# A decode kernel of attention and a token mixer: the query weights in four loads at the head of the queue

## The chip, the core and the metric

The kernel runs on one core of one Trainium2 chip. A core has engines with instruction lists of their own: TensorE (PE in the profile; its weight loads are PEld), VectorE (DVE), ScalarE (ACT), GpSimd (POOL) and SyncE (SP). Sixteen DMA engines bring data from the chip's memory (HBM) into the on-chip memory SBUF, which has 128 rows, here called partitions. A load is issued by one engine's instruction (here nearly always SP's), is split into one packet for each row of its target, and increments a semaphore when it has landed. The engines wait on semaphores for each other.

The metric is the device time of one execution, in microseconds (us). The kernel before takes a median of 1266.54 us in 3 runs (1265.91 to 1266.6).

## What is computed

One decoding step: a row `x` of 448 numbers goes through attention over a long cache and, beside it, through a small mixer; a gate mixes the two.

```python
def _A_ref(x, k_cache, v_cache, wq, wo):        # 16 query heads, 8 key heads, 65536 keys, 256 wide
    q = (x @ wq).reshape(B, Sq, Hq, Dh).transpose(0, 2, 1, 3)
    k = jnp.repeat(k_cache, rep, axis=1)
    v = jnp.repeat(v_cache, rep, axis=1)
    scores = jnp.einsum("bhqd,bhkd->bhqk", q, k) * (Dh ** -0.5)
    p = _softmax(scores, axis=-1)
    o = jnp.einsum("bhqk,bhkd->bhqd", p, v)
    return o.transpose(0, 2, 1, 3).reshape(B, Sq, Hq * Dh) @ wo
...
g = _sigmoid((x * gate_w).sum(-1, keepdims=True))
a = _A_ref(x, A_k_cache, A_v_cache, A_wq, A_wo)
b = _B_ref(x, B_w1, B_b1, B_w2, B_b2)           # layer norm, 448 x 1792 mixer with gelu
return g * a + (1 - g) * b
```

All inputs are bf16. The two caches hold 268 MB each and are read once. The query weights `A_wq` are 448 x 4096 (3.67 MB), the output weights `A_wo` 4096 x 448 (3.67 MB).

## The kernel before

The keys and values are cut into NP = 32 blocks of 16,384 positions, four for each of the 8 key heads. A block of keys or of values is 8.39 MB: 128 partitions of 64 KB. Keys go to a ring `kring` of one and a half blocks, values to one buffer `vbuf`. For each block, PE transposes the keys (L348) into PSUM, VectorE and ScalarE copy them back to SBUF (L656, L796), PE multiplies them by the query (L369), the maximum and the exponential follow, and PE multiplies the weights by the values (L400).

All large loads are on SP's list, in an order written out by hand (L251 to L315), and so go through one queue:

1. `load_wo(0)` (L253, L257): the output weights of the first head pair, 448 KB in 128 rows of 3.5 KB. PE reads them first in `project` (L461), after the first head's four blocks.
2. The big part of the query weights, `wq_a` (L258): rows 0 to 383 of `A_wq`. WF = 3 rows of it go to one partition, so it is 128 rows of 24 KB, 3072 KB. Its place in SBUF is the front of `vbuf`, which the values take over later.
3. The rest of the query weights, `wq_b` (L260): 64 rows of `A_wq`, each cut in two, 128 rows of 4 KB, 512 KB.
4. The first block of keys, in two halves of 4096 KB (L266, L267).
5. From then on values and keys in turn. Each waits for its buffer: keys for transposes (`sem_tr`), values for the products with the block before (`sem_pv`). The first value load (`load_v(0)`, L269) waits for `s_q` (the query is computed, so the query weights may be overwritten) and `s_hb` (L272).

Six small loads are on ACT's list (L759 to L764): the row `x`, the gate's weights, the mixer's weights and biases. At the start, PE turns the row `x` into columns (L481, L484), waits for the small loads, transposes the mixer's weights (L486), waits for VectorE's copy `xcol` (L604) and then, in one wait, for all of the query weights:

```python
pe.wait_ge(s_xcol, 1)
pe.wait_ge(sem_wq, 32)
```

Each load adds 16 to its semaphore, so 32 are two loads. Then 128 small products (L496, L498) give the query, `s_q` is incremented, and the mixer's hidden row is spread over the partitions (L502), which VectorE copies to `hbT` (L723) with `s_hb`.

Of the kernel before, what the change touches and what calls it, by code (L numbers as in the profile page):

```python
# [12 lines left out]
def bass_gated_mix__gqa_block_cached__mixer_token_mlp__decode_kernel(  # L13
# [25 lines left out]
    P = 128  # L39
# [17 lines left out]
    WF = 3  # L57
    REM = DM - WF * P
    assert 0 < REM and 2 * REM == P
    HALF = NQ // 2  # L60

# [32 lines left out]
    with ctx:  # L96
# [6 lines left out]
        def new_sem(name):  # L103
            return ctx.enter_context(nc.semaphore(name))
# [22 lines left out]
        wq_a = early[:, 0:WF * NQ].rearrange("p (j n) -> p j n", j=WF)  # L127
        wq_b = early[:, WF * NQ:WF * NQ + HALF]
        used = [WF * NQ + HALF]

# [71 lines left out]
        sem_wq = new_sem("sem_wq")  # L202
# [43 lines left out]
        def src(cache, j, n0=0, n1=NV):  # L246
            g, m = divmod(j, PPH)
            s = cache[0, g, m * BODY * CH:(m + 1) * BODY * CH, :].rearrange("(p n) d -> p n d", p=P)
            return s[:, n0:n1, :].rearrange("p n d -> p (n d)")

        @block.sync  # L251
        def _(eng):
            def load_wo(g):  # L253
                w = A_wo[g * REP * DH:(g + 1) * REP * DH, :]
                eng.dma_start(wo_rows, w.rearrange("(p i) n -> p (i n)", i=2 * REP)).then_inc(sem_wo, 16)

            load_wo(0)  # L257
            eng.dma_start(wq_a.rearrange("p j n -> p (j n)"),  # L258
                          A_wq[0:WF * P, :].rearrange("(p j) n -> p (j n)", p=P)).then_inc(sem_wq, 16)
            eng.dma_start(wq_b, A_wq[WF * P:DM, :].rearrange("r (a n) -> (r a) n", a=2)  # L260
                          ).then_inc(sem_wq, 16)
            def load(dst, cache, j, n0, n1, at, sem):
                eng.dma_start(dst[:, at + n0:at + n1, :].rearrange("p n d -> p (n d)"), src(cache, j, n0, n1)  # L263
                              ).then_inc(sem, 16)

            load(kring, A_k_cache, 0, HV, NV, 0, sem_k)  # L266
            load(kring, A_k_cache, 0, 0, HV, 0, sem_kb)  # L267

            def load_v(j):  # L269
                if j == 0:  # L270
                    eng.wait_ge(s_q, 1)
                    eng.wait_ge(s_hb, 1)  # L272
                else:
                    eng.wait_ge(sem_pv, j)
                load(vbuf, A_v_cache, j, 0, NV, 0, sem_v)
                g, m = divmod(j, PPH)
                if m == 0 and 1 <= g < H - 1:
                    eng.wait_ge(s_proj, g)
                    load_wo(g)

            for j in range(NP):
                if j == LEAD + 1:
                    eng.wait_ge(sem_tr[NB - 1], BODY * LEAD)
                    load(kring, A_k_cache, j, HV, NV, HV, sem_kc[1])
                if j >= 1:
                    eng.wait_ge(sem_tr[NB - 1], BODY * (j - 1) + DC)
                if j == LEAD:
                    load(kring, A_k_cache, j, HV, NV, 0, sem_k)
                    load(kring, A_k_cache, j, 0, HV, 0, sem_kc[0])
                elif j == LEAD + 1:  # L290
                    load(kring, A_k_cache, j, 0, HV, HV, sem_k)
                elif j == NP - 1:
                    load(kring, A_k_cache, j, 0, HV, HV, sem_k)
                    load(kring, A_k_cache, j, HV, NV, HV, sem_kc[2])
                elif j >= 1:
                    load(kring, A_k_cache, j, 0, NV, HV * (j % 2), sem_k)
                if j < LEAD:
                    load_v(j)
                elif j > LEAD:
                    load_v(j - 1)  # L300


            for (n0, n1), sem in zip(pieces, sem_vp):
                if n0 == 0:
                    eng.wait_ge(sem_tr[NB - 1], BODY * (NP - 1) + DC)
                elif n0 == NRING:
                    eng.wait_ge(sem_pv, NP - 1)
                load(kring if n1 <= NRING else vbuf, A_v_cache, NP - 1, n0, n1, 0, sem)
            eng.wait_ge(s_proj, H - 1)
            for h in range(REP):  # L310
                w = A_wo[(HQ - REP + h) * DH:(HQ - REP + h + 1) * DH, :]
                eng.dma_start(wo_sb[:, h, :], w.rearrange("(p j) n -> p (j n)", j=2)).then_inc(sem_wl[h], 16)
            eng.wait_ge(s_fin, NCG)
            eng.dma_start(out_ap, out_row[:, :]).then_inc(sem_out, 16)
            eng.wait_ge(sem_out, 16)  # L315
# [13 lines left out]
        def _(pe):  # L329
# [95 lines left out]
            def piece_wait(n):  # L425
                for (n0, _), sem in zip(pieces, sem_vp):
                    if n == n0:
                        pe.wait_ge(sem, 16)
# [57 lines left out]
            pe.matmul(acc[:, WF + 2:WF + 2 + 3 * FT], wrows_b, identb, start=True, stop=True).then_inc(s_col, 1)  # L486

            pe.wait_ge(s_xcol, 1)
            pe.wait_ge(sem_wq, 32)
            for dj in range(2):  # L490
                for h in range(HQ):
                    j = dj * HQ + h
                    col = h * DH
                    a, cb = divmod(col, HALF)
                    for kt in range(WF):
# [25 lines left out]
            with nc.Fori(0, NP + 1, 1, engines=on, head_slot={pe.engine: 0}) as jj:  # L521
                j = pe.snap(jj, min_val=0, max_val=NP)
# [312 lines left out]
```

## Time and profile before

| what | value |
|---|---|
| median of 3 runs | 1266.54 us (1265.91 to 1266.6) |
| span of the profiled execution, first to last instruction | 1264.2 us |
| bytes read from HBM | 544.22 MB |
| mean rate over the span | 430 GB/s |
| packets of the DMA engines | 12054 |
| mean granted TensorE clock | 0.859 |

The profile is of one execution; its span leaves out what lies before the first and after the last instruction, and the runs' median is 2.3 us above it. The profile gives each engine's busy time, the span in 40 slices, the DMA queues, a chain of waits followed back from the end, and groups of instructions by source line. A row of the windows view gives a stretch (start and end in us from the span's start), its length, each engine's busy time with the number of instructions, the granted TensorE clock, the busy share of the 16 DMA engines and the GB/s that they moved. A row of the timeline gives start, duration, engine, line, operation, output and inputs, and in brackets what the engine waited for. A row of the waits gives who waited for what, the total in us, how often, and the longest. SPq and ACTq are the lists of SP and ACT from which loads are issued.

### The profile page before, as it was taken

What the parts mean: (1) busy time and instruction counts of PE and PEld (TensorE: products, weight loads), DVE (VectorE), ACT (ScalarE), POOL (GpSimd) and SP (SyncE); (2) the same over time, 40 slices, a digit from 0 to 9 for tenths busy, and PEclk for the clock granted to TensorE, in tenths of its full rate; (3) what the DMA queues carried; (4) which work ended last, traced back from release to release, by engine and by line L of the source; (5) the groups of instructions that cost most, each with busy time, mean ns of one, the idle gap of its engine ahead of it and who ended that gap; (6) DMA issues with size and microseconds to landing.
All of it is one profiled execution on the core that took longest, in us unless ns stands there. A gap on an engine that the chain in (4) does not pass through costs nothing.

```text
span 1264.2 us, 39788 instructions
## 1 busy us (share of the span) xinstructions
PE 955.4 (76%) x17107; PEld 879.2 (70%) x17107; DVE 497.4 (39%) x1124; ACT 544.5 (43%) x691; POOL 0.9 (0%) x7
## 2 busy tenths in 40 slices
PE   4778887778776787767877768876769867698786
PEld 3677876668766687666876657875668756687674
DVE  3333434443543444444344423342333423334342
ACT  2444543345533455333554334443344533345451
POOL 0000000000000000000000000000000000000000
PEclk9878887898888897888987889887888878888898
DMA  9999999999999999999999999999999999999998
GB/s 412 434 421 426 441 431 435 433 431 433 435 433 435 433 431 431 431 440 433 431 435 422 435 435 442 433 425 435 431 431 435 435 433 431 435 431 431 427 448 355
DMA packets 12054, 544.37 MB, mean 431 GB/s; under 512 B 1417, under 2 KB 1676, under 8 KB 2956
## 3 DMA queue, kind: packets, MB, share of 16 engines
q1 hardware_dynamic: 11954, 544.22, 99.7%
q8 instruction: 7, 0.11, 0.0%
q10 hardware_dynamic: 90, 0.01, 0.0%
q14 instruction: 3, 0.02, 0.0%
HBM read 544.22 MB, written 0.00 MB: 430 GB/s over the span
## 4 chain that ended last, share of the span: by engine, by line
DMA 63%; PE 34%; issue 1%; DVE 1%; SPq 0%; DVEq 0%; ACT 0%
DMA kring<-in_A_k_cache_dram 60%; PE kst L348 25%; PE sps L369 6%; DMA vbuf<-in_A_v_cache_dram 2%; PE acc L400 2%; DMA wo_sb<-in_A_wo_dram 1%; PE acc L450 0%; PE sps L388 0%; PE prj L461 0%; SPq L263 0%; PE acc L393 0%; DVE ktT L656 0%; ACT z_b L801 0%; PE sps L386 0%; DVE mrow L667 0%
## 5 line engine op out<-in xcount | busy, mean ns | idle before, releaser
L348 PE MATMUL kst<-ident,kring 128*128 128x128 f32 x4096 | 555.4, 296 | 200.3 <-DMA kring<-in_A_k_cache_dram 177.1
L348 PEld LDWEIGHTS kst<-ident,kring 128*128 128x128 f32 x4096 | 504.1, 154 | 209.2 <-issue 204.1
L796 ACT ACTIVATE ktT<-kst 128x1024 bf16<-128x1024 bf16 x512 | 499.3, 1022 | 348.8 <-PE kst L348 348.0
L656 DVE COPY ktT<-kst 128x1024 bf16<-128x1024 bf16 x512 | 353.9, 692 | 444.0 <-PE kst L348 418.5
L369 PEld LDWEIGHTS sps<-qcur,ktT 128*128 128x128 bf16 x8192 | 237.8, 96 | 2.8 <-issue 0.3
L369 PE MATMUL sps<-qcur,ktT 128*128 128x2 bf16 x8192 | 236.6, 163 | 0.0
L400 PE MATMUL acc<-vbuf,pT 128*2 128x256 bf16 x4008 | 155.2, 328 | 7.2 <-DMA vbuf<-in_A_v_cache_dram 3.6
L400 PEld LDWEIGHTS acc<-vbuf,pT 128*2 128x2 bf16 x4008 | 109.2, 100 | 44.9 <-issue 6.2
L779 ACT ACTIVATE fade<-mdif 128x2 f32<-128x2 f32 x32 | 6.5, 204 | 297.1 <-DVE mdif L673 297.1
L667 DVE TENSOR_REDUCE mrow<-sps 2x1 f32<-2x128 f32 x32 | 8.9, 279 | 156.5 <-PE sps L386 156.5
L388 PEld LDWEIGHTS sps<-mdiag,mones 2*128 2x128 f32 x64 | 11.0, 214 | 27.9 <-DVE mdiag L669 27.9
L783 ACT ACTIVATE pT<-sps,mneg 128x64 f32 x128 | 30.3, 334 | 0.0
L386 PE MATMUL sps<-ident,mcol 128*2 128x128 f32 x32 | 8.9, 279 | 27.7 <-issue 26.2
L388 PE MATMUL sps<-mdiag,mones 2*128 2x2 f32 x64 | 13.7, 282 | 21.3 <-DVE mdiag L669 21.3
L801 ACT ACTIVATE z_b<-z_b 128x448 bf16<-128x448 bf16 x14 | 8.1, 577 | 48.2 <-DVE z_b L643 48.2
L393 PE MATMUL acc<-pT,ones_sq 128*128 128x32 bf16 x256 | 11.9, 181 | 21.8 <-issue 18.3
L386 PEld LDWEIGHTS sps<-ident,mcol 128*2 128x2 f32 x32 | 2.6, 80 | 36.4 <-issue 28.1
L690 DVE COPY accs<-acc 128x288 f32<-128x288 f32 x8 | 3.7, 457 | 60.9 <-PE acc L400 60.9
L662 DVE TENSOR_REDUCE mcol<-sps 128x2 f32<-128x256 f32 x32 | 13.5, 423 | 35.5 <-PE sps L369 35.5
L393 PEld LDWEIGHTS acc<-pT,ones_sq 128*128 128x128 bf16 x256 | 8.7, 99 | 25.8 <-issue 22.2
L685 DVE TENSOR_SCALAR acc<-acc,fader 128x256 f32<-128x256 f32 x32 | 15.8, 493 | 2.5
L672 DVE TENSOR_SCALAR mneg<-sps 128x2 f32<-128x2 f32 x32 | 5.1, 160 | 16.7 <-PE sps L388 16.7
(108 smaller groups left out, 174.6 us busy)
## 6 DMA issues: line engine op xcount, KB each, us to landing
kring<-in_A_k_cache_dram SPq DMA_DIRECT2D x8, 4096.0 KB, 23.8
kring<-in_A_v_cache_dram SPq DMA_DIRECT2D x1, 4608.0 KB, 27.1
wo_sb<-in_A_wo_dram SPq DMA_DIRECT2D x7, 448.0 KB, 25.7
vbuf<-in_A_wq_dram SPq DMA_DIRECT2D x1, 3072.0 KB, 10.4
vbuf<-in_A_v_cache_dram SPq DMA_DIRECT2D x1, 1536.0 KB, 9.2
vbuf<-in_A_v_cache_dram SPq DMA_DIRECT2D x1, 1024.0 KB, 11.3
vbuf<-in_A_v_cache_dram SPq DMA_DIRECT2D x1, 768.0 KB, 12.7
vbuf<-in_A_wq_dram SPq DMA_DIRECT2D x1, 512.0 KB, 11.2
```

Of the source, the lines that this page charges most:

```text
L348: ins = pe.transpose(kst[:, b, i * P:(i + 1) * P], kring_f[:, at + NT * (k % DC) + 4 * b + i, :], ident[:, :])
L369: ins = pe.matmul(sps[:, 0, 2 * (NT * k + nt):2 * (NT * k + nt) + 2], ktT[:, par, b, ntl * DH + dj:(ntl + 1) * DH:2], qcur[:, dj, :], star ...
L386: pe.transpose(mxT, mcol[:, :], ident[:, :]).then_inc(s_mT, 1)
L388: pe.matmul(mxB, mones[:, :], mdiag[:, :], start=True, stop=True).then_inc(s_mB, 1)
L393: pe.matmul(acc[:, DENC:SELC], ones_sq[:, :], pT[:, r, :], start=False, stop=(r == BODY - 1), skip_group_check=True)
L400: ins = pe.matmul(acc[o:o + REP, 0:DH], pT[:, r, 2 * nt:2 * nt + 2], buf[:, n, :], start=False, stop=False, skip_group_check=True)
L656: vec.tensor_copy(ktT[:, k % KTB, b, :], kst_b[:, b, :]).then_inc(sem_ev[b], 1)
L662: vec.tensor_reduce(out=mcol[:, :], in_=scores_all.rearrange("p (n hh) -> p hh n", hh=REP), axis=AX.X, op=ALU.max)
L667: vec.tensor_reduce(out=mrow[:, :], in_=mxT, axis=AX.X, op=ALU.max)
L685: vec.tensor_scalar(acc[:, 0:DENC], acc[:, 0:DENC], fader[:, :], None, op0=ALU.mult).then_inc(s_acc, 1)
L783: ins = act.activation(pT[:, bass.ds(p0, DC), hh:2 * NT:REP], scores_all.rearrange("p (a r n hh) -> p a hh r n", a=2, r=DC, hh=REP)[:, hal ...
L796: act.activation(ktT[:, k % KTB, b, :], kst_b[:, b, :], AF.Copy).then_inc(sem_ev[b], 1)
```

## The change

The load of `wq_a` is cut by partitions into four loads, of partitions 0 to 15, 16 to 31, 32 to 63 and 64 to 127. They are issued ahead of the first output weights instead of behind them. PE's one wait for the query weights counts five loads in place of two.

```diff
     HALF = NQ // 2
+    WQROWS = [(0, 16), (16, 32), (32, 64), (64, P)]
...
+            for p0, p1 in WQROWS:
+                eng.dma_start(wq_a[p0:p1].rearrange("p j n -> p (j n)"),
+                              A_wq[p0 * WF:p1 * WF, :].rearrange("(p j) n -> p (j n)", j=WF)).then_inc(sem_wq, 16)
             load_wo(0)
-            eng.dma_start(wq_a.rearrange("p j n -> p (j n)"),
-                          A_wq[0:WF * P, :].rearrange("(p j) n -> p (j n)", p=P)).then_inc(sem_wq, 16)
             eng.dma_start(wq_b, A_wq[WF * P:DM, :].rearrange("r (a n) -> (r a) n", a=2)
                           ).then_inc(sem_wq, 16)
...
-            pe.wait_ge(sem_wq, 32)
+            pe.wait_ge(sem_wq, 16 * (len(WQROWS) + 1))
```

The data, their places in SBUF and all other loads stay as they are. The four loads carry the same 128 rows of 24 KB. In the changed kernel SP's list begins with loads of 16, 16, 32 and 64 rows of 12288 elements, then the output weights, then `wq_b`, then the two halves of the first keys.

## The prediction

> **What bounds the kernel now.** I read the page's head and busy lines first, then the 40 slices, the queues, the chain, and last the windows of the stretches that the change touches.
>
> ```profile
> span 1264.2 us, 39788 instructions
> ...
> PE 955.4 (76%) x17107; PEld 879.2 (70%) x17107; DVE 497.4 (39%) x1124; ACT 544.5 (43%) x691; POOL 0.9 (0%) x7
> ...
> DMA  9999999999999999999999999999999999999998
> ...
> q1 hardware_dynamic: 11954, 544.22, 99.7%
> ...
> DMA 63%; PE 34%; issue 1%; DVE 1%; SPq 0%; DVEq 0%; ACT 0%
> ```
>
> No engine is busy over 76%. The 16 DMA engines are: the slices show 9 from the first to the last but one, and the packets of SP's queue (q1) take 99.7% of sixteen engines' span. The kernel is one stream of 544.22 MB through one queue, in SP's order. What counts for the end is when the stream starts, how fast it runs, and whether it ever runs dry.
>
> ```profile
> 1.70:1.80 0.10, 0.00 (x0) 0.00 (x0) 0.00 (x0) 0.00 (x0) 0.10 (x1) 1.00 1.76 179
> ...
> 1.50:4.00 2.50, 0.43 (x5) 0.29 (x5) 1.83 (x11) 0.65 (x1) 0.20 (x1) 1.00 0.96 342
> 4.00:12.00 8.00, 0.22 (x1) 0.10 (x1) 2.14 (x8) 0.64 (x1) 0.00 (x0) 1.00 0.96 405
> 12.00:24.00 12.00, 4.92 (x133) 3.94 (x134) 2.97 (x15) 1.69 (x3) 0.00 (x0) 1.00 1.03 440
> ...
> 118.00:119.00 1.00, 0.99 (x9) 1.00 (x10) 0.23 (x1) 0.00 (x0) 0.00 (x0) 1.00 0.55 197
> 119.00:120.00 1.00, 1.00 (x17) 0.99 (x16) 0.89 (x2) 0.81 (x1) 0.00 (x0) 1.00 0.62 262
> ...
> 24.00:1250.00 1226.00, 942.17 (x16803) 870.04 (x16803) 487.70 (x1081) 541.22 (x686) 0.00 (x0) 0.86 1.00 433
> ```
>
> The last two columns are the DMA share and GB/s. Bulk data begin in the stretch 1.7 to 1.8 us, 1.0 us after SP's first issue (0.74, below). The rate is then 433 GB/s over 1226 us: 27.06 GB/s for each of sixteen engines. The one thin place is at 118 to 120 us (197 and 262 GB/s). Where the share passes 1.00, bytes are booked when their packet ends; only sums over long stretches are to be trusted.
>
> ```profile
> PE kst L348 <- DMA kring<-in_A_k_cache_dram: 177.1, 29, 9.7
> ...
> SPq L263 <- PE kst L348: 618.7, 33, 27.1
> SPq L263 <- PE acc L400: 566.0, 30, 29.7
> ...
> SPq L272 <- DVE hbT L723: 14.7, 1, 14.7
> ```
>
> PE waits 177.1 us, 29 times, for keys. SP waits for PE to free buffers, yet its loads stand in a queue that is not empty: a full load is 8.39 MB, 19.4 us at 433 GB/s, and lands a median 27.8 us after its issue (the row kring x28 below), so some 8 us of work is always ahead of it. So a delay or a gain at the head of the stream goes through to the end one for one: the later landings, the transposes behind them and the issues behind those all move together, and the thin place at 118 us (by its two rows 407 KB short of 433 GB/s, at most 0.9 us) moves along too.
>
> **The change part by part.**
>
> ```profile
> 0.73 0.52 ACTq L759 DMA_DIRECT2D vbuf<-in_A_x_dram  x1
> ...
> 0.74 0.41 SPq L255 DMA_DIRECT2D wo_sb<-in_A_wo_dram  x1
> ...
> 1.20 0.42 SPq L258 DMA_DIRECT2D vbuf<-in_A_wq_dram  x1
> ...
> 1.67 0.42 SPq L260 DMA_DIRECT2D vbuf<-in_A_wq_dram  x1
> ...
> 2.13 1.07 SPq L263 DMA_DIRECT2D kring<-in_A_k_cache_dram  x2
> ...
> 17.96 0.33 SPq L263 DMA_DIRECT2D vbuf<-in_A_v_cache_dram  x1
> ```
> ```profile
> vbuf<-in_A_wq_dram SPq DMA_DIRECT2D x1, 3072.0 KB, 10.4
> ...
> kring<-in_A_k_cache_dram SPq DMA_DIRECT2D x28, 27.8
> ```
>
> *Bytes.* The same 448 + 3072 + 512 KB go ahead of the first keys, only in another order. Cost 0.
>
> *Three more issues on SP.* One takes about 0.42 us, one every 0.47: the first keys are issued at 3.5 instead of 2.13. Hidden: the 4.13 MB ahead of them keep the engines busy for 9.5 us. Without that cover it would be 1.4 us. Their extra packets (3 x 16, a few bytes each) I put at 0.03 us; 0 and 0.1 are the bounds.
>
> *Start.* The first load now has one row for each engine. From 1.7 to 4.0 us the stream moved 342 x 2.5 = 855 KB where 433 x 2.3 = 996 KB would go: 0.3 us is lost on first packets of 3.5 KB. Longer first rows and fewer of them can win back up to that, and start up to 1.0 us earlier at the utmost (all that lies between issue and data); at worst nothing. I take -0.2.
>
> *Output weights behind the query weights.* They are first read by L461 at 201.7 us:
>
> ```profile
> L461 PE MATMUL prj<-wo_sb,oTn x8: 257/258/259, 201.7 to 202.0; 128*1 128x224 bf16 x8
> ```
>
> That leaves over 170 us. Cost 0.
>
> *The wait at L489* asks for 80 instead of 32. It is met when the last query weights (wq_b) land, which are the last ahead of the keys in either order; behind it on PE stand the query, then the hidden-row broadcast, and SP's first value load waits for both (the L272 row). That load goes out at 17.96 while the first 8.39 MB of keys are in transfer until about 31 us; both move together. Cost 0, and the cover is some 12 us.
>
> ```profile
> 2.79 0.32 ACTq L764 DMA_DIRECT2D b_b<-in_B_b_dram  x1
> ...
> 11.48 0.10 PEld L486 LDWEIGHTS acc<-vbuf 42*128 42x128 bf16 x1 [8.83 <-DMA b_b<-in_B_b_dram]
> ...
> 13.04 0.22 PE L496 MATMUL sps<-xcol,vbuf 128*128 128x1 bf16 x3 [1.33 <-DMA vbuf<-in_A_wq_dram]
> ```
>
> *ACT's six small loads* share the engines with SP's packets: the last, two bytes, is issued at 2.79 and waited for until 11.48. The query starts at 13.04, when wq_b lands. Slower packets make the small loads later, but once the query weights are through they have only 3.5 and 4 KB packets beside them. Cost 0, covered by wq_b.
>
> *The rows per load.* This is the term that decides. 3072 KB in 128 rows are 24 KB a row; at 27.06 GB/s 0.91 us a row, eight rows an engine, 7.3 us in all. The trace has no load of more than a few KB with fewer than 128 rows, so I bound it. Lower end: what holds the rate at a flat 433 GB/s is the engine; four loads with 1, 1, 2 and 4 rows an engine then take the same 7.3 us: +0. Upper end: what holds it is the place in SBUF, one sixteenth of the path for each eight rows; a load's rate goes with its rows: 16 rows get 54 GB/s, and 393 KB take 7.3 us; so do the other three: 29.1 us, +21.8. That the rate is the same to a GB/s over 1226 us, for 32 KB rows and 64 KB rows alike, says that a fixed path sets it, not which end of that path. No row is nearer to either end, so I take the middle, +10.9: sixteen rows reach more than their eighth of the path, but not all of it.
>
> By the Trainium skill ("SBUF — State Buffer", section "Door 1: The DMA port swizzle") the rate depends on how many of 16 ports the partitions reach, 0 to 15 reaching four (it has 104 GB/s measured, against 328 for all 128), and 32 to 63 and 64 to 127 eight each. By its 109 and 218 GB/s the four loads would take 3.6 + 3.6 + 3.6 + 7.2 = 18.0 us, an estimate, and the sum would be +10.5 instead of +10.7; its advice, one load of 128 partitions, speaks against this change, and no run here shows the rule so far.
>
> *Sum:* +10.9 - 0.2 + 0.03 = +10.7 us on a span of 1264.2: 1274.9. The runs' median is 2.3 us above the span; that part lies outside of the span and stays: 1266.54 + 10.7 = 1277.3.
>
> **The rivals.**
> *Rows don't matter.* Each engine takes one row of 24 KB at its own rate, and only the start changes: -0.2 + 0.03, 1266.4, not slower than before. For it: rows of 24, 32 and 64 KB run at much the same rate (405 in a stretch with the small loads in it, 440, 433). Against: in all of them each engine has eight rows of its own, so the case that matters is not in the trace. It decides where the engine, not its target rows, is the limit. A variant with the same sign: a 16-row load uses fewer than 16 engines, each still getting eight rows in all; the engines of the fourth load start three issues later, +1.4 us, 1267.9.
>
> *Full proportion.* Each eight rows have their own sixteenth: +21.8 - 0.2, 1288.2. For it: the flat ceiling in sixteenths. Against: it needs two to eight engines to queue for the same place from the first packet to the last.
>
> *A faster start.* All that could be won is the 1.0 us before the first data and the 0.3 us after: 1265.2. It cannot leave the 0.2% band.
>
> *Small loads late.* If each of ACT's six loads waited twice, for its data and for its signal, behind a key row (32 KB at 27.06 GB/s, 1.21 us), the query would be 14.5 us late and the first value load with it; 2.5 us beyond its cover, in which the engines idle. With the forecast's 10.7: 1279.8, inside its own range. Against: eight query-weight rows an engine go ahead of the keys, and they take up most of these waits.
>
> **How the numbers follow.** About 0.2%, 2.5 us, is what a measurement of this kernel can tell from no change. Forecast (the middle, 1272 to 1283): 0.66, wide because the share of the path that few rows reach is unknown. Full proportion and what lies near it (1283 to 1289): 0.14. Rows don't matter, with its variant: 0.15. A small loss of 2.5 to 5 us, where engines that queue for one place drift apart and overlap the next load: 0.04. A faster start beyond the band: 0.01. Slower: 0.66 + 0.14 + 0.04 = 0.84; same 0.15; faster 0.01. The range of 8 in 10 leaves out "rows don't matter" and the small loss: 1272 to 1288.5.
>
> **What would show it.** In the first 40 us the stretch of the query weights has some 170 GB/s instead of 405, the first keys land near 34.5 us instead of 23.8 (row below), the value load is issued near 28.6 instead of 17.96; from there on 433 GB/s, and the same thin place, at about 129 us. If the first keys land before 24 us, rows don't matter and the forecast is wrong; near 45 us, full proportion. It is wrong in its second half if the keys land 10 us later and the span grows by much less: then the stream had slack that I didn't see.
>
> ```profile
> 2.13 21.67 DMA kring<-in_A_k_cache_dram
> 23.94 6.40 PE kst L348 x32
> ```

## The result and the profile after

The changed kernel takes a median of 1275.94 us (1275.84 to 1276.3, 5 runs), the kernel before 1266.41 us in 5 runs (1265.62 to 1266.6). The ratio is 1.0078, 95% interval 1.0067 to 1.0089: 9.5 us slower. The forecast was 1277.3.

First the page's head of the changed kernel: busy times, the queue, the rate over the span.

```profile
span 1274.1 us, 39791 instructions
...
GB/s 261 441 434 422 438 430 440 428 432 438 428 438 432 428 440 432 430 438 432 428 442 428 430 440 428 434 424 440 438 434 430 436 432 430 440 430 430 431 437 362
DMA packets 12102, 544.37 MB, mean 427 GB/s; under 512 B 1465, under 2 KB 1724, under 8 KB 3004
...
q1 hardware_dynamic: 12002, 544.22, 99.7%
```

The span is 9.9 us longer. The bytes are the same, and there are 48 more packets, the 3 x 16 of three more loads. The first of the forty slices has 261 GB/s, where it had 412 before; all slices from the second to the last but one lie between 422 and 442, as they lay between 421 and 448 before. The queue is still called 99.7% busy. So the busy share of the DMA engines says nothing of this loss: a packet that takes longer counts as busy for as long as it takes.

Next the windows view of the changed kernel; columns as before, the last three being granted clock, DMA share and GB/s.

```profile
1.50:1.70 0.20, 0.00 (x0) 0.00 (x0) 0.06 (x2) 0.00 (x0) 0.08 (x1) 1.00 0.01 4
1.70:1.80 0.10, 0.00 (x0) 0.00 (x0) 0.00 (x0) 0.00 (x0) 0.10 (x1) 1.00 7.27 1229
...
1.50:22.00 20.50, 0.65 (x6) 0.40 (x6) 4.81 (x21) 1.49 (x2) 0.20 (x1) 1.00 1.00 193
...
24.00:1250.00 1226.00, 958.49 (x16784) 881.58 (x16781) 487.31 (x1079) 540.60 (x681) 0.00 (x0) 0.85 1.00 433
```

The same stretch of the kernel before:

```profile
1.50:22.00 20.50, 5.50 (x138) 4.26 (x138) 6.93 (x32) 2.98 (x4) 0.20 (x1) 1.00 1.02 423
```

All of the loss lies in the first 22 us: 193 GB/s in place of 423, where I had forecast some 170 for the query weights alone; then 433 as before. The thin place, which I looked for near 129 us, is not there (470 GB/s from 128 to 131 us).

The timeline of the loads and of the query's first product, then the first load of keys in the chain of waits, and one of SP's own waits:

```profile
0.73 1.93 SPq L259 DMA_DIRECT2D vbuf<-in_A_wq_dram  x4
...
3.88 0.91 SPq L265 DMA_DIRECT2D kring<-in_A_k_cache_dram  x2
...
20.50 0.10 PEld L488 LDWEIGHTS acc<-vbuf 42*128 42x128 bf16 x1 [17.84 <-DMA b_b<-in_B_b_dram]
...
23.33 0.22 PE L498 MATMUL sps<-xcol,vbuf 128*128 128x1 bf16 x3 [2.61 <-DMA vbuf<-in_A_wq_dram]
...
28.26 0.33 SPq L265 DMA_DIRECT2D vbuf<-in_A_v_cache_dram  x1
```
```profile
3.88 30.47 DMA kring<-in_A_k_cache_dram
```
```profile
SPq L274 <- DVE hbT L725: 23.4, 1, 23.4
```

The first keys land at 3.88 + 30.47 = 34.35 us, 10.5 later than before (23.80). The query starts 10.3 later (23.33 against 13.04), again when wq_b lands and after the small loads are in (20.50). The first value load goes out at 28.26, SP's one wait for the query and the mixer's hidden row being 8.7 us longer; the keys are then still in transfer.

### The profile page after: what moved, and what is told of

Same layout as the page of the kernel before. It is cut to its first block, busy times and chain, and to the rows that moved or that the text cites. A ratio compares the mean times of both kernels' runs of the same rounds, so it can differ in the third digit from the quotient of the medians.

```text
span 1274.1 us, 39791 instructions
## 1 busy us (share of the span) xinstructions
PE 973.5 (76%) x17107; PEld 891.8 (70%) x17107; DVE 497.2 (39%) x1124; ACT 545.0 (43%) x691; POOL 0.9 (0%) x7
## 3 DMA queue, kind: packets, MB, share of 16 engines
q1 hardware_dynamic: 12002, 544.22, 99.7%
## 4 chain that ended last, share of the span: by engine, by line
DMA 60%; PE 36%; issue 2%; DVE 2%; SPq 0%; DVEq 0%; ACT 0%
DMA kring<-in_A_k_cache_dram 57%; PE kst L350 26%; PE sps L371 6%; PE acc L402 3%; DMA vbuf<-in_A_v_cache_dram 2%; DMA wo_sb<-in_A_wo_dram 1%; PE acc L452 0%; PE sps L390 0%; PE prj L463 0%; DVE ktT L658 0%; PE acc L395 0%; SPq L259 0%; ACT z_b L803 0%; SPq L265 0%; PE sps L388 0%
## 5 line engine op out<-in xcount | busy, mean ns | idle before, releaser
L350 PE MATMUL kst<-ident,kring 128*128 128x128 f32 x4096 | 563.7, 299 | 182.5 <-DMA kring<-in_A_k_cache_dram 158.4
L350 PEld LDWEIGHTS kst<-ident,kring 128*128 128x128 f32 x4096 | 511.5, 155 | 191.8 <-issue 185.5
L402 PE MATMUL acc<-vbuf,pT 128*2 128x256 bf16 x4008 | 165.3, 342 | 6.5 <-issue 3.3
L402 PEld LDWEIGHTS acc<-vbuf,pT 128*2 128x2 bf16 x4008 | 114.0, 104 | 49.4 <-issue 5.6
L395 PE MATMUL acc<-pT,ones_sq 128*128 128x32 bf16 x256 | 11.9, 182 | 21.9 <-issue 18.4
```

The source lines that it names most:

```text
L350: ins = pe.transpose(kst[:, b, i * P:(i + 1) * P], kring_f[:, at + NT * (k % DC) + 4 * b + i, :], ident[:, :])
L395: pe.matmul(acc[:, DENC:SELC], ones_sq[:, :], pT[:, r, :], start=False, stop=(r == BODY - 1), skip_group_check=True)
L402: ins = pe.matmul(acc[o:o + REP, 0:DH], pT[:, r, 2 * nt:2 * nt + 2], buf[:, n, :], start=False, stop=False, skip_group_check=True)
```

## The experiments

Ten kernels. The diffs are against the changed kernel. Medians are compared with runs of the kernel before on the same chip.

**The order alone.** One load of 128 rows ahead of the output weights.

```diff
-    WQROWS = [(0, 16), (16, 32), (32, 64), (64, P)]
+    WQROWS = [(0, P)]
```

> The query weights stay one load of 128 rows and go ahead of the first output weights: the order alone. My theory (a load of few partitions reaches only a part of the path into SBUF): 0 +- 0.4 us against before, first keys landing near 23.8 us as before. Rival (the order costs it: query weights first make the small loads or the start late): +9 us as in the changed kernel.

Measured: a ratio of 1.0001 (0.9992 to 1.001). The order costs and gains nothing that can be measured; the interval ends at some 1.3 us. First keys, in the chain of waits of this kernel, at 24.2 us:

```profile
2.13 22.04 DMA kring<-in_A_k_cache_dram
```

**The split alone.** The four loads behind the output weights.

```diff
+            load_wo(0)
             for p0, p1 in WQROWS:
...
-            load_wo(0)
```

> The four loads of 16, 16, 32 and 64 rows, but behind the first output weights: the split alone. My theory: the whole loss, +9.5 to +10.5 us, first keys near 34.5 us. Rival (order): 0.

Measured: 1276.23 us, 1.008 (1.0064 to 1.0095), the whole loss. First keys at 34.6 us (chain of waits):

```profile
3.82 30.75 DMA kring<-in_A_k_cache_dram
```

**Four loads by columns.** As many loads, each over all 128 partitions.

```diff
-    WQROWS = [(0, 16), (16, 32), (32, 64), (64, P)]
+    WQROWS = [(0, 1536), (1536, 3072), (3072, 6144), (6144, WF * NQ)]
...
+            for c0, c1 in WQROWS:
+                eng.dma_start(wq_d[:, c0:c1], wq_p[:, c0:c1]).then_inc(sem_wq, 16)
```

> Four loads again and ahead of the output weights, but each of all 128 partitions, with 1/8, 1/8, 1/4 and 1/2 of the columns (3, 3, 6 and 12 KB rows). My theory (what counts is the partitions reached): 0 +- 0.5 us, first keys near 23.8 us. Rival (each further load costs some 3.3 us, 10 us over three): +10 us.

Measured: a ratio of 1.0008 (0.9999 to 1.0017), first keys at 24.4 us (chain of waits):

```profile
3.84 20.56 DMA kring<-in_A_k_cache_dram
```

The number of loads is not it: of the 10 us that a fixed cost for each load would bring there are at most some 2 (the interval's upper end). The ratio itself, 1 us, lies above the 0.5 us that I had allowed, but the interval reaches no change. Nor is anything won by a small first load.

**Four loads of 32 rows, two of 64, eight of 16.** All of neighbouring partitions.

```diff
+    WQROWS = [(0, 32), (32, 64), (64, 96), (96, P)]
...
+    WQROWS = [(0, 64), (64, P)]
...
+    WQROWS = [(16 * i, 16 * i + 16) for i in range(8)]
```

> Four loads of 32 rows each. My theory with the Trainium skill's port map (32 neighbouring partitions reach 8 of 16 ports): 4 x 3.6 to 3.9 us instead of 7.3, +7 to +8.5 us, first keys near 31 to 32 us. Rival, rate in proportion to the rows: 32 rows at a quarter, 29 us, +21.8. Rival, a fixed cost for each load: as in the changed kernel, +9.5 to +10.

> Two loads of 64 rows each. My theory with the port map (partitions 0 to 63 and 64 to 127 reach 8 of 16 ports each): 2 x 7.3 us, +7 us, the same as four loads of 32. Rival, a fixed cost of 3.3 us for each further load: +3.3. Rival, neighbouring rows in HBM: +7 too; this run doesn't tell that one apart.

> Eight loads of 16 neighbouring rows. My theory with the port map (4 of 16 ports each): 8 x 3.3 to 3.6 us, +19 to +21.5 us. Rate in proportion to the rows: 8 x 7.3 us, +51. A fixed cost for each further load: +23.

Measured: four of 32: 1273.69 us, 1.0061 (1.0045 to 1.0076); two of 64: 1274.06 us, 1.0059 (1.0042 to 1.0076); eight of 16: 1285.12 us, 1.0144 (1.0127 to 1.0161). Against the kernel before that is +7.8, +7.3 and +18.4 us, the last a little under my +19 to +21.5. Two loads cost as much as four, so it isn't a cost for each load (that would be +3.3 and +10); 32 rows run as fast as 64, so it isn't in proportion to the rows. The windows view shows it directly. From the middle of the query weights, one row for each kernel, in the order above. The DMA share, next to last, is 1.00 to 1.05, so all sixteen engines are at work in each case and every packet takes longer:

```profile
5.00:15.00 10.00, 0.00 (x0) 0.00 (x0) 1.83 (x7) 0.13 (x1) 0.00 (x0) 1.00 1.05 217
```
```profile
5.00:15.00 10.00, 0.00 (x0) 0.00 (x0) 0.79 (x4) 0.25 (x1) 0.00 (x0) 1.00 1.04 215
```
```profile
5.00:25.00 20.00, 0.22 (x1) 0.10 (x1) 2.27 (x10) 0.87 (x2) 0.00 (x0) 1.00 1.00 114
```

Half of 433 is 217, a quarter 108. Loads of 32 and of 64 neighbouring rows run at half of the rate, loads of 16 at a quarter and a little.

**Other sets of partitions.** Eight loads of 16 rows, every eighth partition; four of 32 rows, every fourth.

```diff
+    WQROWS = [(i, P, 8) for i in range(8)]
...
+    WQROWS = [(i, P, 4) for i in range(4)]
...
+                eng.dma_start(wq_a[p0:p1:st].rearrange("p j n -> p (j n)"), wq_p[p0:p1:st, :]).then_inc(sem_wq, 16)
```

> Eight loads of 16 rows again, but each takes every eighth partition (0, 8, ... 120; then 1, 9, ...). Port map: such a set reaches 8 ports, 2 engines on each, 8 x 1.8 us, +7 us. If eight neighbouring partitions had a path of their own: each load reaches all sixteen, 0 to +0.5 us. A fixed cost for each load: +23. HBM neighbours: here the source rows are spread too, so 0.

> Four loads of 32 rows, each of every fourth partition (0, 4, ... 124; then 1, 5, ...). By the port map each such load reaches all 16 ports. If the reach of the load alone counts: 0 to +0.5 us. If what counts is how many engines write to one port at the same time, and neighbouring rows of the load go to the same engine (two rows each, so that 8 ports are in use at any time): 4 x 3.7 us, +7 us, as with 32 neighbouring rows.

Measured: every eighth 1273.63 us, 1.0056 (1.0039 to 1.0073); every fourth 1266.04 us, 0.9999 (0.999 to 1.0009), no measurable loss with 32 rows a load. The same view, every eighth first:

```profile
5.00:15.00 10.00, 0.21 (x1) 0.10 (x1) 3.15 (x16) 1.69 (x3) 0.00 (x0) 1.00 1.04 217
```
```profile
4.00:9.00 5.00, 0.00 (x0) 0.00 (x0) 1.72 (x6) 0.72 (x1) 0.00 (x0) 1.00 0.93 395
```

Sixteen rows get 114 GB/s as neighbours and 217 at every eighth partition; thirty-two get 217 as neighbours and the full rate at every fourth: 395 GB/s at a DMA share of 0.93, where the kernel with the order alone has 419 at 0.98 in the same stretch. It is which partitions, not how many.

**The source.** The four targets of the changed kernel, their rows taken from all over the query weights.

```diff
...
+            for (p0, p1), r0 in zip(WQROWS, (0, 1, 2, 1)):
+                st = P // (p1 - p0)
+                eng.dma_start(wq_a[p0:p1].rearrange("p j n -> p (j n)"), wq_p[r0:P:st, :]).then_inc(sem_wq, 16)
```

> The same four targets as in the changed kernel (partitions 0 to 15, 16 to 31, 32 to 63, 64 to 127), but the source rows of each load lie spread over the query weights, 8, 8, 4 and 2 rows of 24 KB apart; so some partitions get other rows' weights and some rows are read twice or not at all. My theory (the target limits): +9.5 to +10.5 us, as in the changed kernel. Rival (the source limits: engines that read neighbouring rows of HBM get in each other's way): 0 to +1.

Measured: 1276.0 us, 1.0074 (1.0057 to 1.0091), the changed kernel's time to 0.1 us. In the stretch of the load of 64 rows it and the changed kernel (the second row) have the same rate:

```profile
13.00:19.00 6.00, 0.00 (x0) 0.00 (x0) 0.00 (x0) 0.00 (x0) 0.00 (x0) 1.00 0.96 197
```
```profile
13.00:19.00 6.00, 0.00 (x0) 0.00 (x0) 0.00 (x0) 0.00 (x0) 0.00 (x0) 1.00 0.96 197
```

Spreading the rows of the source changes nothing; the target does.

**Two queues.** The halves of 64 rows, one from SP's list and one from ACT's.

```diff
-    WQROWS = [(0, 16), (16, 32), (32, 64), (64, P)]
+    WQROWS = [(0, 64), (64, P)]
...
-            for p0, p1 in WQROWS:
+            for p0, p1 in WQROWS[:1]:
...
             act.dma_start(xrow_b, x_row_ap).then_inc(sem_x, 16)
+            for p0, p1 in WQROWS[1:]:
+                act.dma_start(wq_a[p0:p1].rearrange("p j n -> p (j n)"),
+                              A_wq[p0 * WF:p1 * WF, :].rearrange("(p j) n -> p (j n)", j=WF)).then_inc(sem_wq, 16)
```

> Two loads of 64 rows, partitions 0 to 63 from SP's list and 64 to 127 from ACT's, behind the row x, so that packets for both halves are in the queues at the same time. If an engine that waits for its port can't take the other list's packet: most of the loss of two loads stays, +5 to +7 us. If the engines share out between the halves, both sets of 8 ports are in use: +0.5 to +3 us. The other small loads of ACT stand behind its half and land some 8 us later, which the wait for the last query weights covers.

Measured: 1273.93 us, 1.0066 (1.0049 to 1.0083), +8.2, above both of the ranges that I gave: nothing is won back, although SP issues its half at 0.73 us and ACT its own at 1.30. The window from 5 to 15 us:

```profile
5.00:15.00 10.00, 0.00 (x0) 0.00 (x0) 0.80 (x4) 0.70 (x1) 0.00 (x0) 1.00 0.97 206
```

With packets for both halves in the queues the sixteen engines still move half of the rate. The queue rows of the DMA view say which half they are at; a row gives the packets that start in the stretch, their MB, and their time as a share of sixteen engines. SP's queue is q1, ACT's is q10. First 2 to 7 us, then 7 to 12 us:

```profile
q1 hardware_dynamic: 48, 1.18, 106.2%
```
```profile
q10 hardware_dynamic: 30, 0.74, 68.8%
q1 hardware_dynamic: 24, 0.39, 36.8%
```

Up to 7 us only SP's half is in transfer; ACT's half begins as SP's ends. So the halves go mostly one behind the other, and this run has them side by side for at most some 5 us, in which both queues together move 1.13 MB, 226 GB/s. Why the engines take the halves in turn, and why nothing is won where both are in transfer, the trace doesn't show.

## Why the prediction came out right

*What bounds the kernel: right.* A stream through one queue, in which a delay at its head reaches the end. The keys came 10.5 us late, the span grew by 9.9. From the landing of the first keys to the end the kernel before takes 1240.4 us, the changed kernel 1239.8, and the ten variants 1239.8 to 1240.8: "one for one" holds within 1 us, over delays of up to 19.6 us (eight loads of 16).

My step "the thin place moves along" was wrong: it went away, and its two rows had made it too large. The view books a packet whole where it starts (below), so a row of 1 us is scattered by packets of 64 KB, which take longer than that (2.4 us at 27.06 GB/s); the kernel before has 229 GB/s from 124 to 125 us too, and 524 in the next microsecond. Spread over the time that each packet took, the packets of the trace before move 399 and 317 GB/s in the two microseconds from 118 to 120, some 0.3 us short of 433 and not 0.9; those of the changed kernel move 432 and 431. That is about half of the 0.6 us. The rest is no larger than the scatter among the variants, and its cause stays open.

*The rows per load: right in mechanism for these four loads, and in size by luck.* The target holds the rate, and 16 or 32 neighbouring rows reach only a part of the path, but more than their share of it: that is what the runs show. What the prediction doesn't have is that the number of rows is not what counts, since 32 rows at every fourth partition reach all of it. The size was the middle, +10.9, between the engine as the limit (+0) and eight rows for each sixteenth of the path (+21.8), taken because no row lay nearer to either. Measured at the first keys it is +10.5. The trace of before could not bear that out, and that the measured loss lay at the middle was luck. Both ends fell. "Rows don't matter" falls with every split by neighbouring partitions. "Full proportion" fell too: it would have 16 neighbours at 54 GB/s, and they have 114; by it 64 rows would run at twice the rate of 32, and they run at the same, 215 and 217.

What stands in their place is the law that the last paragraph of that part weighed. The Trainium skill ("SBUF — State Buffer", section "Door 1: The DMA port swizzle") gives each partition to one of 16 ports: neighbours in fours, partitions 32 to 63 on the same eight ports as 0 to 31, and 64 and up on the other eight. By it 16 neighbours reach four ports, 32 or 64 eight, every eighth partition eight, every fourth all sixteen. The traces agree in each case: 114; 217 and 215; 217; and 395 in a stretch with the small loads in it, with no loss in the runs. The estimate from its figures for the four loads, 18.0 us in place of 7.3, is +10.7 for the rows alone, beside +10.5 at the keys. Its measured 104 GB/s for 16 partitions is 9% below this kernel's 114, and here the 114 counts.

*The start, -0.2: wrong, nothing in its place.* Data begin between 1.7 and 1.8 us in the changed kernel too, and the three variants that keep the full rate, by order, columns or every fourth partition, are at ratios of 1.0001, 1.0008 and 0.9999: a first load of fewer rows, or of fewer bytes, won nothing that can be measured. The row from 1.70 to 1.80 also corrects how I read that view: 1229 GB/s and a share of 7.27 in a tenth of a microsecond can only be packets booked whole where they start, not where they end as the prediction has it. They are five rows of 24 KB, 123 KB, with 11.6 us of packet time, 2.3 us each; had they ended there, they would have started before SP's first issue at 0.73. Two numbers of the prediction were read from short rows and hang on this: the 0.9 us of the thin place and the 0.3 us that bounds the start.

*What I put at nothing: right.* The first keys were issued at 3.88 instead of 3.5 us, under the same cover. The small loads landed 9 us later, at 20.5, before wq_b at 23.3, so the rival "small loads late" did not come up. The value load went out at 28.26 against 28.6 forecast. The output weights behind the query weights cost nothing: the order alone shows it.

*The 1.2 us between the forecast loss (10.7 us) and the measured one (9.5)* are 0.4 of the rows less 0.2 of the start, 0.6 lost between the keys and the end, and 0.4 by which the medians moved less than the spans, each of these from one profiled execution. The 0.4 comes from the "2.3 us above the span" of the sum, which set the median of three runs beside the span of another execution: in every run on record with its own span the time is 1.75 to 1.85 us above it.

## What to carry to other kernels

Cut a load by columns, or take every fourth partition, before cutting it into blocks of neighbouring partitions: the same bytes in blocks of 32 or 64 neighbours ran at half of the rate, in blocks of 16 at a quarter, and in a kernel that is one stream of loads this goes through to the end. A busy share of the DMA engines near 1 doesn't show it; look at the GB/s of the stretch. And where a trace has no row for a shape, a forecast from it is a range between two mechanisms: find the run that tells them apart. Here it is eight loads of 16 rows, for which the mechanisms gave 0, some 20, 23 and 51 us.

## What was not expected

Every fourth partition, 32 rows a load, ran at the full rate: I had set +7 us beside 0 there, for the case that neighbouring rows of a load go to one engine and so to one port in turn. The other is the two queues: I had expected the loss to shrink a little even if the engines didn't share out between the halves, and it is +8.2 us, no smaller than that of two loads from one list (+7.3).
